# Softmax reciprocals on GpSimd's power instead of VectorE, in a fused attention and gated-MLP kernel

## The chip, the cores and the metric

The kernel runs on one core of one Trainium2 chip. The metric is the time of one execution on the device in microseconds (us). A core has TensorE (matrix products; PE, and PEld for its weight loads), VectorE (DVE), ScalarE (ACT), GpSimd (POOL) and SyncE (SP, which here only issues DMAs). Each works through its own instructions in order, and they wait for each other on semaphores.

## The reference

One input x of 2048 tokens by 512 channels goes through a layernorm, and three things are added: x itself, a sliding-window attention, and a gated MLP whose gate mixes tokens.

```python
xn = layernorm(x)
# attention: 32 heads of 16, each token looks at 8 tokens: itself and 2, 4, ... 14 before it
q, k, v = xn @ wqkv
logits  = einsum('bhsd,bhswd->bhsw', q, k_gathered) * 16 ** -0.5    # masked before token 0
attn    = softmax(logits)                                           # over the 8
A       = einsum('bhsw,bhswd->bhsd', attn, v_gathered) @ wo
# gated MLP
z  = gelu(xn @ w_in);  z1, z2 = z[..., :896], layernorm(z[..., 896:])
g  = einsum('ts,bsf->btf', w_sp, z2) + b_sp                         # 2048 x 2048
B  = (z1 * g) @ w_out
out = x + A + B
```

The matmuls take bf16 operands, with fp16 in some sums.

## The kernel before

The kernel is a list of tasks. Each task names its engine, the buffers that it reads and writes, an estimated duration (`est`, in ns) and a function that issues one or a few instructions. From the buffers the planner works out what must wait for what. The order of the tasks on each engine is written out by hand in `plan.orders`: five lists, for TensorE, ScalarE, VectorE, GpSimd and SyncE. The estimates only settle what the lists leave open.

Tokens are kept in 16 blocks of 128. The work goes through these stages:

- Layernorm of x (`bnst`, `bnag`, `rstd`, `norm`). `rstd` is a GpSimd power of one element per partition: the variance to the power -0.5 (line 657).
- Products with w_in and wqkv (`z2_`, `Q`, `K`, `z1_`, `V`). For the attention's logits VectorE multiplies Q with shifted K (`prod`, line 758) and adds up (`padd`, line 766); TensorE sums over the channels of a head (`lg`).
- The layernorm of z2, in four waves of four blocks (`zm`, `zq`, `ze`, `zv`, `zr`, `zb`, `zn`). `zr` is a GpSimd power of four elements per partition (line 934); `zb` (line 936, VectorE) reads its result.
- The softmax, in four groups of 512 tokens, 3 first and 0 last. VectorE takes the maximum over the eight window positions (`sm1`, `sm2`, `sm3`), subtracts it (`ssub`), ScalarE takes the exponential (`sexp`), VectorE adds the eight (`sz1`, `sz2`, `sz3`), takes the reciprocal of the sum (`srec`, line 847, 128 partitions by 128 sums) and multiplies (`sattn`).
- The spatial product with w_sp, in eight tiles of two output blocks. It is a fast scheme with seven products (`P1` to `P7`, 8 matmuls each) instead of eight; VectorE makes sums of z2 (`T1` to `T4`, line 962) and, for each tile, sums of the weights (`S13`, `S2`, `S4`, lines 982 to 988). It also takes two of the four results out of the PSUM (`g12`, `g22`) and multiplies the gate with z1 (`u`). A DMA transposes each `u` (`uT`).
- Beside each tile VectorE does the attention's weighted sum of V for two blocks: `pv` (line 1163), then halving sums `pva2048`, `pva1024` (line 1167) and `pvc` (line 1171), then a DMA transposes the result (`OTd`).
- The output blocks `out15` to `out0` on TensorE (lines 1225 and 1229) take the transposed attention times wo and the transposed `u` times w_out, onto x.

The sums Z and the reciprocals R of the softmax have one buffer each, shared by the four groups. So `sz3` of a group waits until the reciprocal of the group before it has read Z, and a reciprocal waits until `sattn` of the group before it has read R. In VectorE's list of before, the reciprocal of a group stands between its `sz3` and its `sattn`; group 3 comes at about 102 us, group 2 at 113, group 1 at 163 and group 0 at 189.

Of the kernel before, what the change touches and what calls it, by code (L numbers as in the profile page):

```python
# [14 lines left out]
class Plan:  # L15
# [291 lines left out]
ALU = mybir.AluOpType  # L307
ACTF = mybir.ActivationFunctionType
# [18 lines left out]
def build_kernel(nc, A_x, A_wqkv, A_wo, B_x, B_w_in, B_w_sp, B_b_sp, B_w_out, out, report=False, sched_kw=None,  # L327
                 cfg=None, emit=True):
    cfg = dict(DEFAULT_CFG, **(cfg or {}))
# [10 lines left out]
    FILL = cfg["fill"]  # L340
# [65 lines left out]

    foff = {}
    fb = 0
    for name, n in (("prime", 4), ("Z", 128), ("st6", NB * 9),
                    ("mv", NB * 2), ("rstd", NB), ("s1", 2 * NB), ("s2", NB), ("m2", NB), ("msq", NB),  # L410
                    ("rstd2", NB), ("nb2", NB), ("mhalf", 4), ("bias", NB), ("P5s", 2 * HF)):
        foff[name] = fb
        fb += n
    F32_E = fb
# [3 lines left out]
    with ExitStack() as es:  # L418
# [10 lines left out]
        def A(name, n, o2_=0):  # L429
            return ar[:, off[name] + o2_: off[name] + o2_ + n]  # L430
# [16 lines left out]
        R = plan.reg  # L447
# [101 lines left out]
        zeros = A("zeros", 512)  # L549
        maskt = A("maskt", 32)  # L550
        hm = A("hm", 32)
        mhalf = Fv("mhalf", 4)
# [53 lines left out]
        for which, eng in ((0, "sp"), (1, "sp")):  # L606
# [4 lines left out]
                writes=[(("wq", "wk")[which], c) for c in range(4)],  # L611
                name="ld%s" % ("qk"[which]))
# [7 lines left out]
        def filler(n, name, est, prio=None, reads=(), w=512):  # L620
# [6 lines left out]

        filler(cfg["warm"], "warm", 114.0 * cfg["warm"], w=146)

        T("act", lambda a: a.activation(Fv("prime", 4), mhalf, ACTF.Gelu_apprx_tanh), reads=["mhalf"], writes=["prime"],  # L630
          est=-1200, name="actprime", tbl="gelu")

        ring = [0]
# [201 lines left out]
        def softmax_tail(j):  # L835
# [4 lines left out]
              reads=[dk], writes=["Za"], est=c_dve(512, 2.0), name="sz1_%d" % j, prio=FILL)  # L840
            T("dve", lambda v: v.tensor_tensor(AC(off["Zb"], [[64, 4], [1, 64]]), AC(off["Za"], [[128, 4], [1, 64]]),
                                               AC(off["Za"] + 64, [[128, 4], [1, 64]]), ALU.add),
              reads=["Za"], writes=["Zb"], est=c_dve(256, 2.0), name="sz2_%d" % j, prio=FILL)
            T("dve", lambda v: v.tensor_tensor(FCa(foff["Z"], [[32, 4], [1, 32]]), AC(off["Zb"], [[64, 4], [1, 32]]),
                                               AC(off["Zb"] + 32, [[64, 4], [1, 32]]), ALU.add),
              reads=["Zb"], writes=["Z"], est=c_dve(128), name="sz3_%d" % j, prio=FILL)
            T("dve", lambda v: v.reciprocal(A("R", 128), Fv("Z", 128)), reads=["Z"], writes=["R"], est=960,
              name="srec%d" % j, prio=FILL)
            dv = AC(off["attn"] + d0, [[256, 4], [32, 8], [1, 32]])
            T("dve", lambda v: v.tensor_tensor(dv, dv, AC(off["R"], [[32, 4], [0, 8], [1, 32]]), ALU.mult),  # L850
              reads=["R"], writes=[dk], est=c_dve(1024, 2.0), name="sattn%d" % j, prio=FILL)
# [226 lines left out]
        for j in range(NJ):  # L1078
# [18 lines left out]
            if j == 1:  # L1097
# [5 lines left out]
                  name="biasf")  # L1103
# [141 lines left out]
        for t in range(NT):  # L1245
# [11 lines left out]
            if t >= 1:  # L1257
# [4 lines left out]
        plan.orders = [  # L1262
            """
                warm xTr0b fill0 xTr0a z2_0_0b z2_0_1b z2_0_0a xTr1a xTr1b z2_0_1a xNr z2_1_0a z2_1_0b z2_1_1a xTr2a
                xTr2b z2_1_1b z2_2_0a z2_2_0b xTr3a z2_2_1a xTr3b z2_2_1b z2_3_0a z2_3_1a z2_3_1b z2_3_0b K0_0 K0_3
                K0_1 Q0_1 K0_2 Q0_0 Q0_2 Q0_3 K1_0 Q1_0 Q1_1 Q1_2 K1_1 K1_2 K1_3 Q1_3 z2_4 z2_5 z2_6 z2_7 Q2_0 K2_0
                Q2_1 K2_1 Q2_2 K2_2 Q2_3 K2_3 z2_8 z2_10 z2_9 z2_11 Q3_1 K3_1 K3_0 K3_2 Q3_2 Q3_0 z2_12 z2_13 K3_3
                lg0_0 Q3_3 z1_14 z2_15 z2_14 z1_12 z1_13 z1_15 z1_11 z1_8 z1_10 z1_6 z1_7 z1_9 z1_5 z1_4 z1_2 z1_0
                z1_3 z1_1 V12 V13 V15 V14 lg2_0 V9 V10 V11 V6 V7 V4 V3 V8 V5 V1 V0 V2 P1_0 P5_0 P6_0 P2_0 P7_0 bits
                P3_0 P1_1 P4_0 P5_1 P6_1 P2_1 P3_1 P7_1 P1_2 P4_1 P2_2 P6_2 P5_2 P7_2 P3_2 out15_0 P4_2 out14_0 P1_3  # L1270
                P5_3 P6_3 P2_3 P7_3 P3_3 P1_4 P4_3 P5_4 P2_4 out13_0 P6_4 out12_0 P7_4 P3_4 out11_0 P1_5 P5_5 P4_4
                P6_5 out10_0 P2_5 P7_5 P3_5 P1_6 P4_5 out8_0 P6_6 P2_6 P5_6 P7_6 P3_6 P1_7 out9_0 out6_0 P5_7 P4_6
                out7_0 P6_7 out4_0 P3_7 P7_7 P2_7 out5_0 P4_7 out3_0 out2_0 out0_0 out1_1 out1_0 out1_2
            """.split(),
            """
                actprime ldw_in2a_1 ldw_in2b_1 ldx2 ctr0 xTe0b xTe0a xTe1a xTe1b xNe z2g0_0 xTe2a xTe2b z2g0_1 z2g1_0
                xTe3a xTe3b z2g2_1 z2g1_1 z2g2_0 z2g3_0 z2g3_1 z2s0 QKe0_1 z2s1 QKe0_0 QKe0_2 QKe0_3 z2s2 halo0_0
                QKe1_0 halo1_0 halo0_2 halo0_3 QKe1_1 QKe1_2 z2s3 halo1_1 QKe1_3 biasf halo0_1 z2g4 z2s4 z2g5 z2g6
                z2s5 z2g7 z2s6 QKe2_0 QKe2_1 z2s7 QKe2_2 QKe2_3 halo1_3 zn2 z2g8 halo1_2 z2g10 z2s8 halo2_2 z2g9 z2g11
                z2s9 QKe3_1 halo2_3 z2s10 QKe3_2 QKe3_0 z2s11 z2g12 z2g13 z2s12 lge0 QKe3_3 lge1 halo2_1 z1g14 z2g15  # L1280
                zn3 z2g14 z2s13 z1g12 z1g13 z2s14 z1g15 halo2_0 z1g11 zn6 z1g8 zn7 z1g10 z1g6 z2s15 z1g7 z1g9 zn1 z1g5
                zn4 z1g4 z1g2 zn0 z1g0 zn8 z1g3 zn5 Ve12 Ve13 zn9 Ve15 z1g1 lge2 lge3 Ve9 Ve10 Ve11 Ve14 zn10 zn11 Ve7
                Ve6 ldxr0 Ve8 Ve4 sexp3 Ve5 Ve2 cA_0 Ve1 Ve3 Ve0 cB_0 g11_0 sexp2 cE_0 cA_1 g21_0 cE_1 cB_1 g11_1
                sexp1 cA_2 g21_1 os14_0 os15_0 cB_2 cE_2 g21_2 g11_2 cA_3 cB_3 ldxr2 ldxr1 cE_3 fin15_0 g11_3 cA_4
                fin14_0 os13_0 os12_0 g21_3 cE_4 sexp0 fin13_0 cB_4 fin12_0 os11_0 ldxr3 st0_0_0 os10_0 ldxr4 st1_0_0
                g11_4 cA_5 g21_4 cB_5 fin10_0 fin11_0 os8_0 os9_0 g11_5 ldxr5 cE_5 cA_6 g21_5 cB_6 os6_0 fin8_0
                st2_0_0 os7_0 g11_6 cE_6 cA_7 fin9_0 ldxr6 os4_0 st3_0_0 g21_6 fin6_0 fin7_0 os5_0 cB_7 fin4_0 os2_0
                cE_7 os3_0 st4_0_0 g11_7 ldxr7 fin5_0 g21_7 fin3_0 os0_0 os1_1 st5_0_0 fin2_0 os1_0 st6_0_0 fin0_0
                os1_2 fin1_0 st7_0_0 fin1_2 st7_1_384
            """.split(),  # L1290
            """
                zeros steps0 steps1 bnst0 bnag0 ctr1 bnst1 bnag1 norm0 norm1 bnst2 bnag2 bnst3 norm2 bnag3 norm3 bnst5
                bnag5 norm5 bnst6 bnag6 bnst4 bnag4 bnst7 norm6 bnag7 norm4 bnst10 zm0_0 norm7 bnag10 zm0 zq0 bnst11
                bnst8 bnag11 bnst9 bnag8 prod0_1 prod0_0 bnag9 norm10 norm8 bnst14 norm11 bnag14 padd0_0 bnst12 norm9
                bnst13 bnag12 bnag13 bnst15 prod0_2 norm14 bnag15 padd0_1 ze0 norm12 zv0 norm13 prod0_3 zm1 norm15
                padd0_2 zb0 prod1_2 prod1_0 padd1_0 zq1 padd1_1 ze2 prod2_0 zm2 ze1 prod2_2 zv1 zq2 padd2_0 zb1 zv2
                prod3_2 padd2_1 zm3 prod3_0 zq3 ze3 zb2 padd3_0 zv3 T3_0 padd3_1 smask T1_0 T3_1 S13_0 T2_0 zb3 zn12
                zn13 zn14 T1_1 S2_0 zn15 S4_0 T3_3 T4_0 T2_1 T1_3 sm1_3 T2_3 sm2_3 sm3_3 T3_2 ssub3 T1_2 T4_3 T2_2
                T4_1 T4_2 sz1_3 sz2_3 sz3_3 sm1_2 srec3 sm2_2 sattn3 sm3_2 pv15 ssub2 pv14 sz1_2 g22_0 sz2_2 g12_0
                S13_1 sz3_2 S2_1 u14 sm1_1 srec2 S4_1 pva2048_0 sm2_1 u15 sm3_1 pva1024_0 ssub1 g12_1 g22_1 u12 pvc0  # L1300
                S13_2 sz1_1 S2_2 sattn2 S4_2 sz2_1 u13 pv12 pv13 sm1_0 sz3_1 g22_2 pva2048_1 sm2_0 g12_2 pva1024_1
                S13_3 pvc1 S2_3 pv11 pv10 S4_3 pva2048_2 u11 g22_3 S13_4 sm3_0 g12_3 u10 pva1024_2 S2_4 ssub0 S4_4
                pvc2 u8 pv9 pv8 sz1_0 pva2048_3 S13_5 pva1024_3 g22_4 pvc3 srec1 g12_4 u9 u6 sattn1 S2_5 pv6 pv7 S4_5
                sz2_0 pva2048_4 u7 pva1024_4 g22_5 sz3_0 pvc4 S13_6 g12_5 S2_6 pv4 pv5 S4_6 pva2048_5 u4 u5 pva1024_5
# [66 lines left out]
```

## Time and profile before

| | |
|---|---|
| median of 3 runs | 226.86 us (226.82 to 228.16) |
| profiled execution | 226.98 us, span 225.2 us |
| TensorE busy | 220.8 us (98%), granted clock 1.0 |
| VectorE busy | 209.0 us (93%), 246 instructions |
| ScalarE busy | 135.4 us (60%) |
| GpSimd busy | 36.2 us (16%), the last instruction at 84.6 us |
| VectorE reciprocals | 4, mean 950 ns |
| GpSimd powers of 128x1 | 16, mean 1056 ns (548 to 2571) |
| GpSimd powers of 128x4 | 4, mean 4303 ns (3330 to 5201) |

The span runs from the first to the last instruction of the profiled execution. Busy time is the time in which an engine has an instruction under way, which says nothing of what it waits for inside an instruction. Matmuls are pipelined, and their ends are modelled. VectorE's instructions are recorded with an overlap of some 0.08 us, so the step from one start to the next is a little shorter than a duration.

### The profile page before, as it was taken

The page shows a single profiled execution, that of the slowest core. Times are in us where ns is not written, and L with a number is a line of the kernel's source. Part 1 is how long each engine was busy: PE and PEld are TensorE (multiplying, and loading weights), DVE is VectorE, ACT ScalarE, POOL GpSimd, SP SyncE. Part 2 cuts the span into 40 slices and gives each one's busy share as a digit, 9 for nine tenths or more (in the row PEclk, how much of TensorE's full clock was granted, in tenths as well). Part 3 has the DMA queues.
Part 4 walks back from the last instruction along what each step waited for, and adds up shares of the span by engine and source line. Part 5 has one row for each costly group of instructions (what it writes and reads, how often), then busy time and mean ns, then how long its engine had stood idle before and what let it go on. Part 6 is the DMA issues. An engine that isn't in the chain of part 4 may idle for free.

```text
span 225.2 us, 3118 instructions
## 1 busy us (share of the span) xinstructions
PE 220.8 (98%) x1162; PEld 122.1 (54%) x1176; DVE 209.0 (93%) x246; ACT 135.4 (60%) x241; POOL 36.2 (16%) x35
## 2 busy tenths in 40 slices
PE   8999999999999999999999999999999999999995
PEld 6555555554677775665454445554454555444444
DVE  4699999999998999999999999999999999999910
ACT  4679899899999999985434211362425241244342
POOL 4445595000079106000000000000000000000000
PEclk9999999999999999999999999999999999999999
DMA  6995365850000005669997989849955994507272
GB/s 220 260 197 141 71 188 117 136 122 0 0 3 0 0 0 166 139 119 273 199 204 156 183 156 204 203 94 180 231 123 111 221 176 95 140 0 162 75 162 93
DMA packets 77400, 29.96 MB, mean 133 GB/s; under 512 B 68669, under 2 KB 75339, under 8 KB 77259
## 3 DMA queue, kind: packets, MB, share of 16 engines
q1 hardware_dynamic: 74250, 25.08, 54.2%
q10 hardware_dynamic: 3136, 4.69, 6.2%
q8 instruction: 9, 0.15, 0.3%
q14 instruction: 5, 0.04, 0.1%
HBM read 9.05 MB, written 2.10 MB: 49 GB/s over the span
## 4 chain that ended last, share of the span: by engine, by line
PE 56%; DVE 35%; issue 5%; POOL 2%; ACT 1%; DVEq 0%
PE ps L1023 32%; DVE arena L758 14%; PE ps L1229 11%; DVE arena L766 8%; PE ps L1225 6%; DVE arena L962 4%; PE ps L883 3%; POOL fpool L934 2%; PE ps L624 2%; PE ps L735 2%; DVE arena L1163 1%; DVE fpool L652 1%; DVE arena L982 1%; DVE arena L667 1%; DVE arena L945 1%
## 5 line engine op out<-in xcount | busy, mean ns | idle before, releaser
L1023 PE MATMUL ps<-arena 128*128 128x448 f16 (+1 forms) x448 | 87.3, 353 | 0.3 <-DVE arena L982 0.2
L1023 PEld LDWEIGHTS ps<-arena 128*128 128x128 f16 (+1 forms) x448 | 43.4, 98 | 42.6 <-DVE arena L1069 0.8
L1163 DVE TENSOR_TENSOR arena<-arena 128x4096 bf16<-128x4096 bf16 x16 | 36.0, 2291 | 0.0
L758 DVE TENSOR_TENSOR arena<-arena 128x8192 bf16<-128x8192 bf16 (+1 forms) x10 | 35.5, 3563 | 0.3 <-ACT arena L743 0.3
L1038 ACT ACTIVATE ps<-ps 128x448 f32<-128x448 f32 x16 | 8.4, 528 | 35.4 <-DVE arena L1065 17.8
L1167 DVE TENSOR_TENSOR arena<-arena 128x4096 bf16<-128x4096 bf16 (+1 forms) x16 | 28.1, 1757 | 0.0
L735 PE MATMUL ps<-arena 128*128 128x512 bf16 x123 | 27.7, 379 | 0.4 <-issue 0.2
L1229 PE MATMUL ps<-arena 128*128 128x512 bf16 (+2 forms) x125 | 26.9, 355 | 0.1
L766 DVE TENSOR_TENSOR arena<-arena 128x4096 bf16<-128x4096 bf16 (+1 forms) x9 | 26.9, 2987 | 0.0
L903 PE MATMUL ps<-arena 128*128 128x448 bf16 x128 | 24.5, 352 | 0.0
L934 POOL TENSOR_TENSOR fpool<-fpool 128x4 f32<-128x4 f32 x4 | 17.2, 4303 | 37.2 <-DVE fpool L928 26.3
L1041 ACT ACTIVATE arena<-ps,fpool 128x448 bf16<-128x448 f32 x16 | 10.0, 631 | 20.5 <-PE ps L1023 19.1
L903 PEld LDWEIGHTS ps<-arena 128*128 128x128 bf16 x128 | 18.5, 144 | 5.9
L735 PEld LDWEIGHTS ps<-arena 128*128 128x128 bf16 x128 | 14.4, 113 | 13.2 <-issue 0.4
L657 POOL TENSOR_TENSOR fpool<-fpool 128x1 f32<-128x1 f32 x16 | 16.8, 1056 | 13.6 <-DVE fpool L655 13.1
L1238 ACT ACTIVATE arena<-ps 128x512 bf16<-128x512 f32 (+2 forms) x17 | 9.4, 560 | 15.6 <-PE ps L1229 15.6
L860 PE MATMUL ps<-arena 128*128 128x448 bf16 x96 | 18.8, 352 | 0.0
L1229 PEld LDWEIGHTS ps<-arena 128*128 128x128 bf16 x126 | 11.9, 98 | 12.4
L743 ACT ACTIVATE arena<-ps 128x1024 bf16<-128x1024 f32 x16 | 15.9, 1022 | 3.1 <-PE ps L735 3.1
L1225 PE MATMUL ps<-arena 128*128 128x512 bf16 (+2 forms) x66 | 15.5, 353 | 0.3
L915 ACT ACTIVATE arena<-arena 128x896 bf16<-128x896 bf16 x16 | 15.2, 949 | 0.1
L909 ACT ACTIVATE arena<-ps 128x896 bf16<-128x896 f32 x16 | 14.3, 911 | 0.4 <-PE ps L903 0.2
(85 smaller groups left out, 243.4 us busy)
## 6 DMA issues: line engine op xcount, KB each, us to landing
arena<-in_A_x_dram ACTq DMA_DIRECT2D x8, 256.0 KB, 3.4
arena<-in_A_x_dram SPq DMA_DIRECT2D x15, 128.0 KB, 2.5
out_dram<-arena ACTq DMA_DIRECT2D x7, 256.0 KB, 3.1
arena<-arena SPq DMA_DIRECT2D x1, 1568.0 KB, 9.2
arena<-in_A_wqkv_dram SPq DMA_DIRECT2D x3, 512.0 KB, 4.6
arena<-in_B_w_in_dram SPq DMA_DIRECT2D x1, 896.0 KB, 4.9
arena<-in_B_w_out_dram SPq DMA_DIRECT2D x1, 896.0 KB, 5.1
arena<-arena SPq DMA_TRANSPOSE x40, 3.2
```

The costliest lines, as they stand in the source:

```text
L657: T("pool", lambda g: g.tensor_tensor(Fv("rstd", 1, b), Fv("mv", 1, 2 * b + 1), Fv("mhalf", 1), ALU.pow), reads=[("mv", b), "mhalf"], writ ...
L735: last = t.matmul(bank(k + which), AC(off["wqk"] + 1024 * dc + col0, [[4, 128]]), AC(off["xnT"] + dc * S + 512 * j, [[1, 512]]), start=(dc ...
L758: T("dve", lambda v: v.tensor_tensor(pbv, qb, kb, ALU.mult), reads=[(t_, c, j) for t_ in ("QT", "KT", "KTpad") for c in cs], writes=[("pb" ...
L766: T("dve", lambda v: v.tensor_tensor(av, av, bv, ALU.add), reads=[("pb", s_) for s_ in b], writes=[("pb", s_) for s_ in a], est=c_dve(4096 ...
L860: last = t.matmul(ps[:, 512 * (k + hf): 512 * (k + hf) + HF], AC(off["xnT"] + dc * S + 128 * b, [[1, 128]]), AC(off["w_in2"] + FH * dc + H ...
L903: lastm = t.matmul(ps[:, 512 * (k + hf): 512 * (k + hf) + HF], AC(off["xnT"] + dc * S + b, [[NTOK, 128]]), AC(off["w_in1"] + FH * dc + HF ...
L934: T("pool", lambda g: g.tensor_tensor(Fv("rstd2", 4, 4 * j), Fv("msq", 4, 4 * j), mhalf, ALU.pow), reads=[("msq", j), "mhalf"], writes=[(" ...
L1023: last = t_.matmul(pb_(k_), st(k), mv(k), start=(start and k == 0), stop=(k == 7), skip_group_check=True)
L1163: T("dve", (lambda iv, tv, av: lambda v: v.tensor_tensor(tv, iv, av, ALU.mult))(iv, tv, av), reads=[("attn", q // 4)] + [("V", i_) for i_ ...
L1167: T("dve", (lambda n: lambda v: v.tensor_tensor(AC(off["Vs"], [[4096, 2], [1, n]]), AC(off["Vs"], [[4096, 2], [1, n]]), AC(off["Vs"] + n, ...
L1225: t_.matmul(po, AC(off["OT"] + 1024 * (t % 3) + 512 * r_ + 128 * cc, [[1, 128]]), AC(off["wo"] + 512 * cc + c0, [[1, n]]), start=False, st ...
L1229: last = t_.matmul(po, AC(off["z1"] + FH * tb + 128 * fc, [[1, 128]]), AC(off["w_out"] + 512 * fc + c0, [[1, n]]), start=False, stop=(fc = ...
```

## The change

For groups 0, 1 and 2 the reciprocal becomes a GpSimd power with exponent -1: the exponent is a constant -1.0 in one new fp32 element per partition, read 128 times. Group 3 keeps VectorE's reciprocal. To make room, the buffer of the priming activation shrinks by two columns. The planner's estimate for the power is 20 us. All five lists are new, and were made with longer durations for the z2 powers than before; GpSimd's now ends with `srec2 srec1 srec0`, and VectorE's leaves a stretch of other work between `sz3` and `sattn` of these groups.

```diff
@@ DEFAULT_CFG
+    rpool=(0, 1, 2),
@@ build_kernel
-    for name, n in (("prime", 4), ("Z", 128), ("st6", NB * 9),
+    for name, n in (("prime", 2), ("Z", 128), ("st6", NB * 9),
...
-                    ("rstd2", NB), ("nb2", NB), ("mhalf", 4), ("bias", NB), ("P5s", 2 * HF)):
+                    ("rstd2", NB), ("nb2", NB), ("mhalf", 4), ("mone", 1), ("bias", NB), ("P5s", 2 * HF)):
...
+        T("pool", lambda g: g.memset(Fv("mone", 1), -1.0), writes=["mone"], est=110, name="mone", prio=2)
...
@@ softmax_tail
-            T("dve", lambda v: v.reciprocal(A("R", 128), Fv("Z", 128)), reads=["Z"], writes=["R"], est=960,
-              name="srec%d" % j, prio=FILL)
+            if j in cfg["rpool"]:
+                T("pool", lambda g: g.tensor_tensor(A("R", 128), Fv("Z", 128), FCa(foff["mone"], [[0, 128]]), ALU.pow),
+                  reads=["Z", "mone"], writes=["R"], est=20000, name="srec%d" % j)
+            else:
+                T("dve", lambda v: v.reciprocal(A("R", 128), Fv("Z", 128)), reads=["Z"], writes=["R"], est=960,
+                  name="srec%d" % j, prio=FILL)
@@ plan.orders, VectorE, around the moved steps (before)
-  ... S13_1 sz3_2 S2_1 u14 sm1_1 srec2 S4_1 pva2048_0 sm2_1 u15 sm3_1 pva1024_0 ssub1 g12_1 g22_1 u12 pvc0
-  S13_2 sz1_1 S2_2 sattn2 ... sm1_0 sz3_1 g22_2 ... pvc3 srec1 g12_4 u9 u6 sattn1 ...
-  sz3_0 pvc4 ... pva1024_5 srec0 S13_7 sattn0 ...
@@ the same (after)
+  ... sz3_2 sm1_1 S13_1 g12_0 sm2_1 S2_1 sm3_1 pv14 u14 ssub1 S4_1 pva2048_0 g22_1 sz1_1 S13_2 g12_1 S2_2 pva1024_0 u15 pvc0
+  S4_2 sz2_1 u12 u13 sm1_0 pv12 pv13 g12_2 sz3_1 pva2048_1 g22_2 sattn2 pva1024_1 S13_3 ... pv8 pv9
+  sattn1 pva2048_3 sz1_0 g22_4 sz2_0 pva1024_3 sz3_0 S13_5 g12_4 S2_5 u9 pvc3 u6 pv6 pv7 S4_5 pva2048_4
+  S13_6 pva1024_4 g22_5 S2_6 g12_5 S4_6 pvc4 u7 pv5 pv4 u4 pva2048_5 sattn0 ...
@@ plan.orders, GpSimd (after)
+  ... rstd12 rstd14 zr0 zr1 zr2 mask1 zr3 srec2 srec1 srec0
```

More of the change, by code (lines that the diff above doesn't have):

```diff
@@ L628, in build_kernel @@
         filler(cfg["warm"], "warm", 114.0 * cfg["warm"], w=146)
-        T("act", lambda a: a.activation(Fv("prime", 4), mhalf, ACTF.Gelu_apprx_tanh), reads=["mhalf"], writes=["prime"],
+        T("act", lambda a: a.activation(Fv("prime", 2), Fv("mhalf", 2), ACTF.Gelu_apprx_tanh), reads=["mhalf"], writes=["prime"],
           est=-1200, name="actprime", tbl="gelu")
@@ L1264, in build_kernel @@
                 warm xTr0b fill0 xTr0a z2_0_0b z2_0_1b z2_0_0a xTr1a xTr1b z2_0_1a xNr z2_1_0a z2_1_0b z2_1_1a xTr2a
[L1265 to L1273, printed above, removed]
+                xTr2b z2_1_1b z2_2_0a z2_2_0b xTr3a z2_2_1a xTr3b z2_2_1b z2_3_0a z2_3_1a z2_3_1b z2_3_0b K0_0 K0_1
+                K0_3 Q0_0 K0_2 Q0_1 Q0_2 Q0_3 K1_0 Q1_1 K1_1 Q1_0 K1_2 Q1_2 z2_4 Q1_3 K1_3 z2_7 z2_5 z2_6 K2_2 K2_0
+                Q2_0 K2_1 Q2_1 Q2_3 K2_3 Q2_2 z2_8 z2_10 z2_9 z2_11 K3_1 Q3_1 Q3_0 K3_2 Q3_2 K3_0 z2_12 z2_13 Q3_3
+                K3_3 lg0_0 z1_14 z2_15 z2_14 z1_13 z1_12 z1_15 z1_11 z1_8 z1_6 z1_10 z1_7 z1_5 z1_9 z1_2 z1_0 z1_4 V13
+                z1_1 V12 z1_3 V10 lg2_0 V11 V14 V15 V7 V6 V8 V4 V9 V5 V1 V2 V0 V3 P1_0 P5_0 P6_0 P2_0 P7_0 bits P3_0
+                P4_0 P1_1 P5_1 P6_1 P2_1 P7_1 P3_1 P1_2 P4_1 P6_2 P2_2 P5_2 P3_2 P7_2 P1_3 out14_0 P2_3 P4_2 out15_0
+                P6_3 P5_3 P7_3 P3_3 P1_4 P4_3 out12_0 P5_4 P2_4 P6_4 out13_0 P7_4 P3_4 out11_0 P4_4 P1_5 out10_0 P6_5
+                P5_5 P2_5 P7_5 P3_5 P1_6 P5_6 P4_5 P6_6 out8_0 P3_6 P2_6 P7_6 out9_0 P1_7 out6_0 P6_7 P5_7 P4_6 P7_7
+                P3_7 P2_7 out7_0 out5_0 out4_0 P4_7 out2_0 out3_0 out0_0 out1_1 out1_0 out1_2
             """.split(),
@@ L1276, in build_kernel @@
                 actprime ldw_in2a_1 ldw_in2b_1 ldx2 ctr0 xTe0b xTe0a xTe1a xTe1b xNe z2g0_0 xTe2a xTe2b z2g0_1 z2g1_0
[L1277 to L1289, printed above, removed]
+                xTe3a xTe3b z2g2_0 z2g2_1 z2g3_1 z2g1_1 z2g3_0 z2s0 z2s1 QKe0_0 z2s2 QKe0_1 QKe0_2 z2s3 QKe0_3 QKe1_1
@@ new lines, in build_kernel @@
+                QKe1_0 halo0_1 halo0_2 halo1_1 QKe1_2 halo0_3 z2g4 QKe1_3 z2s4 z2g7 halo0_0 z2g5 z2s5 z2g6 z2s6 QKe2_0
+                z2s7 QKe2_1 halo1_0 halo1_2 QKe2_3 QKe2_2 z2g8 halo1_3 z2s8 z2g10 z2g9 halo2_3 z2s9 z2g11 z2s10 QKe3_1
+                zn2 QKe3_2 QKe3_0 halo2_1 z2s11 z2g12 z2g13 zn7 QKe3_3 lge0 z2s12 z1g14 zn1 halo2_0 z2g15 z2g14 z2s13
+                z1g13 z1g12 zn6 z1g15 z1g11 z2s14 z1g8 z2s15 z1g6 halo2_2 lge1 z1g10 z1g7 biasf zn4 z1g5 z1g9 zn11 zn3
+                z1g0 z1g2 z1g4 zn9 Ve13 z1g1 Ve12 zn8 z1g3 zn10 lge2 lge3 Ve14 Ve11 Ve10 Ve15 zn0 Ve7 ldxr1 ldxr0 Ve8
@@ new lines, in build_kernel @@
+                Ve6 zn5 Ve9 Ve4 Ve2 Ve5 sexp3 cA_0 Ve1 cE_0 Ve3 Ve0 cB_0 sexp2 g11_0 cA_1 cB_1 os15_0 g11_1 cE_1 sexp1
+                cA_2 g21_0 cB_2 g21_1 cE_2 os14_0 g11_2 cA_3 fin15_0 fin14_0 cB_3 g11_3 cE_3 os12_0 ldxr2 st0_0_0
+                g21_2 cA_4 sexp0 g21_3 os13_0 cB_4 fin12_0 fin13_0 os10_0 os11_0 cE_4 ldxr4 ldxr3 g11_4 fin11_0 cA_5
+                cB_5 fin10_0 g21_4 st2_0_0 cE_5 os6_0 g11_5 os8_0 os9_0 st1_0_0 cA_6 cB_6 fin8_0 os7_0 ldxr6 ldxr5
+                cE_6 g11_6 g21_5 fin9_0 st3_0_0 cA_7 fin6_0 cB_7 os4_0 cE_7 os5_0 g21_6 ldxr7 fin7_0 g11_7 st4_0_0
@@ L1290, in build_kernel @@
+                os2_0 fin5_0 fin4_0 st5_0_0 os0_0 g21_7 os3_0 fin2_0 fin3_0 os1_1 os1_0 st6_0_0 fin0_0 os1_2 fin1_0
+                st7_0_0 fin1_2 st7_1_384
             """.split(),
             """
-                zeros steps0 steps1 bnst0 bnag0 ctr1 bnst1 bnag1 norm0 norm1 bnst2 bnag2 bnst3 norm2 bnag3 norm3 bnst5
-                bnag5 norm5 bnst6 bnag6 bnst4 bnag4 bnst7 norm6 bnag7 norm4 bnst10 zm0_0 norm7 bnag10 zm0 zq0 bnst11
-                bnst8 bnag11 bnst9 bnag8 prod0_1 prod0_0 bnag9 norm10 norm8 bnst14 norm11 bnag14 padd0_0 bnst12 norm9
@@ L1295, in build_kernel @@
[L1295 to L1304, printed above, removed]
@@ L1305, in build_kernel @@
-                srec0 S13_7 sattn0 g22_6 pvc5 g12_6 pv2 pv3 S2_7 pva2048_6 S4_7 pva1024_6 u3 pvc6 u2 pv1 pv0 g12_7
-                g22_7 pva2048_7 u0 pva1024_7 pvc7 u1 fin1_1
+                zeros steps0 steps1 bnst0 bnag0 ctr1 bnst1 bnag1 norm0 norm1 bnst2 bnag2 bnst3 norm2 bnag3 norm3 bnst4
+                bnag4 norm4 bnst6 bnag6 bnst5 norm6 bnag5 bnst7 bnag7 norm5 zm0_0 bnst9 norm7 bnag9 zm0 bnst8 zq0
+                bnst10 bnag8 bnag10 prod0_0 prod0_1 norm8 bnst11 norm9 bnag11 ze0 padd0_0 norm10 bnst12 norm11 bnst15
@@ new lines, in build_kernel @@
+                bnst13 bnag15 bnag13 prod0_2 zv0 bnag12 padd0_1 bnst14 norm13 prod0_3 zm1 bnag14 norm15 norm12 padd0_2
+                norm14 zq1 ze1 prod1_2 zv1 prod1_0 zb0 zm2 padd1_0 zb1 zq2 padd1_1 prod2_0 ze2 prod2_2 zm3 zv2 padd2_0
+                zq3 prod3_0 ze3 prod3_2 zb2 padd2_1 zv3 padd3_0 padd3_1 zn15 zn14 smask zn13 zn12 T3_2 S13_0 T1_2 S2_0
+                T2_2 T3_3 T1_3 T4_2 T3_0 T2_3 T4_3 S4_0 T1_0 sm1_3 T3_1 sm2_3 sm3_3 ssub3 T2_0 T1_1 T2_1 T4_0 T4_1
+                sz1_3 sz2_3 sm1_2 sz3_3 sm2_2 srec3 sm3_2 zb3 sattn3 ssub2 pv15 g22_0 sz1_2 sz2_2 sz3_2 sm1_1 S13_1
@@ new lines, in build_kernel @@
+                g12_0 sm2_1 S2_1 sm3_1 pv14 u14 ssub1 S4_1 pva2048_0 g22_1 sz1_1 S13_2 g12_1 S2_2 pva1024_0 u15 pvc0
+                S4_2 sz2_1 u12 u13 sm1_0 pv12 pv13 g12_2 sz3_1 pva2048_1 g22_2 sattn2 pva1024_1 S13_3 sm2_0 S2_3 sm3_0
+                pvc1 S4_3 ssub0 u10 pv11 pv10 g22_3 pva2048_2 u11 S13_4 g12_3 S2_4 pva1024_2 u8 pvc2 S4_4 pv8 pv9
+                sattn1 pva2048_3 sz1_0 g22_4 sz2_0 pva1024_3 sz3_0 S13_5 g12_4 S2_5 u9 pvc3 u6 pv6 pv7 S4_5 pva2048_4
+                S13_6 pva1024_4 g22_5 S2_6 g12_5 S4_6 pvc4 u7 pv5 pv4 u4 pva2048_5 sattn0 pva1024_5 g12_6 pvc5 S13_7
@@ L1307, in build_kernel @@
+                g22_6 S2_7 pv2 pv3 u5 S4_7 pva2048_6 u2 pva1024_6 u3 pvc6 g12_7 pv0 pv1 u0 g22_7 pva2048_7 pva1024_7
+                pvc7 u1 fin1_1
             """.split(),
             """
-                mhalf ident0 ident1 nident0 nident1 ktpad rstd0 rstd1 rstd2 rstd3 mask0 hm0 hm1 rstd5 hm2 rstd6 rstd4
-                rstd7 mask1 rstd10 rstd8 rstd11 rstd9 rstd14 rstd13 rstd12 rstd15 zr0 zr1 zr2 zr3
+                mhalf ident0 mone ident1 nident0 nident1 ktpad rstd0 rstd1 rstd2 rstd3 hm0 mask0 rstd4 rstd6 hm1 rstd5
@@ L1311, in build_kernel @@
+                rstd7 rstd9 hm2 rstd8 rstd10 rstd11 rstd13 rstd15 rstd12 rstd14 zr0 zr1 zr2 mask1 zr3 srec2 srec1
+                srec0
             """.split(),
             """
-                ldx0 ldx1 ldw_in2a_0 ldw_in2b_0 ldx3 ldx5 ldx6 ldx4 ldx7 ldk ldx10 ldx11 ldq ldx9 ldx8 xTd5 xTd6 xTd4
-                xTd7 ldx14 ldx13 ldx15 ldb ldx12 xTd10 xTd11 xTd8 xTd9 ldw_in1 xTd12 xTd13 w0_0 xTd15 xTd14 ldwv w0_1
-                ldwout Vzero pT3 pT2 pT1 pT0 w1_0 w1_1 Vhaloa w2_0 w2_1 Vhalob ldwo1 ldwo0 ldwo2 ldwo3 uT15 OTd0 uT14
@@ L1316, in build_kernel @@
-                w3_0 w3_1 uT13 uT12 w4_1 w4_0 OTd1 w5_0 w5_1 uT11 OTd2 uT10 uT8 w6_0 uT9 OTd3 w6_1 w7_0 uT6 uT7 w7_1
-                OTd4 uT4 uT5 OTd5 uT3 uT2 OTd6 uT0 OTd7 uT1 st7_1_192 st7_1_0
+                ldx0 ldx1 ldw_in2a_0 ldw_in2b_0 ldx3 ldx4 ldx6 ldx5 ldk ldx7 ldx9 ldq ldx8 ldx10 xTd4 xTd6 xTd5 xTd7
+                ldx11 ldx12 ldx15 ldb ldx14 ldx13 xTd9 xTd8 xTd10 xTd11 ldwv w0_0 xTd13 xTd15 xTd12 xTd14 ldw_in1 w0_1
+                ldwout pT3 pT2 Vzero pT0 pT1 w1_0 w1_1 Vhalob ldwo0 ldwo1 ldwo2 w2_0 w2_1 Vhaloa ldwo3 uT14 w3_0 OTd0
@@ L1318, in build_kernel @@
+                uT15 w3_1 w4_0 uT12 uT13 OTd1 w4_1 w5_0 uT10 uT11 OTd2 w5_1 w6_0 uT8 w6_1 uT9 OTd3 uT6 w7_0 OTd4 w7_1
+                uT7 uT4 uT5 OTd5 uT3 uT2 OTd6 uT0 OTd7 uT1 st7_1_192 st7_1_0
             """.split(),
```

## The prediction

> **What bounds the kernel now.** I read the busy shares first, then the table by stretches, the chain of waits, the groups of lines 657, 847 and 934, and last the timelines of VectorE and GpSimd side by side.
>
> ```profile
> PE 220.8 (98%) x1162; PEld 122.1 (54%) x1176; DVE 209.0 (93%) x246; ACT 135.4 (60%) x241; POOL 36.2 (16%) x35
> ...
> PE 56%; DVE 35%; issue 5%; POOL 2%; ACT 1%; DVEq 0%
> ...
> 105.00:125.00 20.00, 19.70 (x104) 9.63 (x103) 20.00 (x29) 8.21 (x13) 0.00 (x0) 1.00 1.02 204
> 125.00:145.00 20.00, 19.95 (x103) 10.02 (x103) 20.00 (x19) 4.84 (x9) 0.00 (x0) 1.00 0.85 180
> 145.00:165.00 20.00, 19.89 (x101) 9.88 (x102) 20.00 (x24) 7.64 (x13) 0.00 (x0) 1.00 0.77 175
> 165.00:185.00 20.00, 19.95 (x103) 10.08 (x103) 20.00 (x21) 7.43 (x15) 0.00 (x0) 1.00 0.75 148
> ```
>
> The stretch columns are length, then busy time and count of PE, PEld, DVE, ACT and POOL, then granted clock, DMA share and GB/s. From 105 us on, where the reciprocals in question stand, TensorE and VectorE are both full, and GpSimd does nothing. The chain's last 111 us is TensorE work without a gap, but each spatial product needs a weight sum (S13, S2, S4) that VectorE has just made. Set side by side, product P5 of tile 1 starts 0.05 us after its S13 ends, P6 of tiles 1 and 2 start 0.59 and 0.05 us after their S2, P3 of tile 3 starts 0.81 us after its S4. So neither engine has room: a stall of VectorE reaches TensorE within about 1 us, and work taken from VectorE alone can at most close the 1.3 us that TensorE idles between its first matmul (0.84) and its last end (222.96; busy 220.8).
>
> At the end the two meet again:
>
> ```profile
> 213.57 0.69 DVE L1171 TENSOR_TENSOR arena<-arena 128x1024 bf16<-128x1024 bf16 x1
> ...
> 214.29 1.23 SPq L1175 DMA_TRANSPOSE arena<-arena  x1
> ...
> 217.95 1.03 PE L1225 MATMUL ps<-arena 128*128 128x512 bf16 x4
> ```
>
> The last pvc sum ends at 214.26, its transpose is issued at once and lands 3.2 us later (median of these transposes), at about 217.5, and the output block that needs it starts at 217.7 to 217.95. VectorE's end has some 0.2 us of room before it moves the end of the kernel.
>
> **What a power costs.** A VectorE reciprocal stands in the groups at 0.95 us; start to next start it is 0.86 (102.15 to 103.01). No power of 128x128 is in the trace. The nearest rows are those of 128x1 and 128x4, beside VectorE's tensor_tensor of the same moment:
>
> ```profile
> 23.93 2.24 DVE L766 TENSOR_TENSOR arena<-arena 128x4096 bf16<-128x4096 bf16 x1
> ...
> 24.09 2.49 POOL L657 TENSOR_TENSOR fpool<-fpool 128x1 f32<-128x1 f32 x1 [1.01 <-DVE fpool L655]
> ...
> 68.82 4.42 DVE L758 TENSOR_TENSOR arena<-arena 128x8192 bf16<-128x8192 bf16 x1
> 73.16 2.29 DVE L766 TENSOR_TENSOR arena<-arena 128x4096 bf16<-128x4096 bf16 x1
> ...
> 63.43 5.20 POOL L934 TENSOR_TENSOR fpool<-fpool 128x4 f32<-128x4 f32 x1 [26.28 <-DVE fpool L928]
> 68.98 5.12 POOL L934 TENSOR_TENSOR fpool<-fpool 128x4 f32<-128x4 f32 x1 [0.35 <-DVE fpool L932]
> ```
>
> Read the ends, not the durations. The 128x1 power ends at 26.58, 0.41 us after the VectorE sum ends (26.17). The 128x4 power of 68.98 ends at 74.10, 0.87 us after the product before it ends (73.24). So the long spans are waits: a power gets nothing done while a VectorE tensor_tensor with two inputs in the SBUF runs. Behind its end, one element per partition takes 0.41 us and four take 0.87, that is (0.87 - 0.41) / 3 = 0.153 us per further element. A power of 128 elements is then 0.41 + 127 x 0.153 = 19.9 us. Bounds: 0.41 if length cost nothing, which the four-element row excludes, and 128 x 0.87 / 4 = 27.8 if it went at that row's mean. I take 19.9, the slope.
>
> **The change part by part.**
>
> Removed from VectorE: three reciprocals, 3 x 0.86 = 2.6 us.
>
> New lists: the second z2 power no longer holds VectorE up (0.90 us before line 936 in the waits; the new list puts a product, two tiny steps and a sum in between): 0.9 us. The rest of the lists reorders the same work. Adding up VectorE's list with the steps of the trace, S13 of tile 1 comes 2.3 us sooner, S2 of tile 2 3.7 sooner, S13 of tile 5 1.9 later, the last pvc and u 2.6 sooner (just the reciprocals). With TensorE full I count nothing for it.
>
> Added in the set-up: one memset of 128x1 on GpSimd, some 0.10 us like its neighbours there, before the first rstd power, for which GpSimd waits 1.8 us anyway. A priming activation of two columns instead of four: nothing.
>
> Moved: srec2, srec1, srec0 go to GpSimd's queue, last in it, so nothing queues behind them there but each other. They issue no DMA, and SP's queue isn't crossed; its transposes and TensorE follow VectorE's end. VectorE gets waits: sz3 of the next group writes Z, which the power reads, and sattn reads R. Behind sattn stand pv, S and u steps, all for TensorE. The new list puts cover there: between sz3 and sattn stand 24.8 us of VectorE steps for group 2, 24.1 for group 0, and 22.9 for group 1 (counted from sattn2, whose R must be read first); sz3_1 comes 21.8 us after sz3_2. Against 19.9 us plus a wait for the instruction in progress (up to 2.3) that is just enough. Without the cover each power would cost 19.9 - 0.86 us.
>
> What it does to VectorE meanwhile is the step that decides. The rows show that a power cannot read while a tensor_tensor reads. On a shared path the other direction must hold too while the power reads, and the cover consists of tensor_tensors. How long does the power read? The lower end: with four elements the hold cannot be seen beyond 0.15 us (a 128x32 sum at 87.14 takes 0.32 us, tiny sums around it 0.15 to 0.17), and the 73.16 sum keeps its 2.29 us while the power computes till 74.10. So reads run at least four elements ahead of the arithmetic, and the write-back collides with nothing. Were all 128 read ahead at that rate, the hold would be 32 x 0.15 = 4.8 us at most, and 0.15 us at least. The upper end: the whole 19.9. A read-ahead has to be stored somewhere, and 128 elements of two operands are 32 times what the row shows; I let it run 16 ahead, four times the row. The hold is then (128 - 16) x 0.153 = 17.1 us, nearer the long end.
>
> [...]
>
> **The sum.** Three holds of 17.1 us: +51.4. Reciprocals -2.6, z2 wait -0.9, room at the end -0.2. TensorE cannot run ahead by more than its 1 us, and it has kept its slack as the end is set by VectorE's last steps. Together +47.7 us. The profiled execution took 226.98 us (span 225.2 and 1.8 around it), so 274.7 us; the runs' median of 226.86 is 0.1 us lower, which I leave out.
>
> **The rivals.**
>
> (a) *No hold worth seeing; not slower.* Reads run ahead of the arithmetic by all 128 elements, or are given up whenever VectorE asks. For it: the four-element rows hold VectorE for 0.15 us at most. Against: 32 times as much must be stored or re-requested. Then the covers hide the powers, VectorE gains up to 3.5 us, and TensorE, full, lets at most 1.3 of it through: 225.7 to 227, say 226.3. It holds as long as a power stays under its cover of 21.8 to 24.8 us. Chance 0.25.
>
> (b) *The power is starved instead.* It reads in small pieces, and each piece waits for the VectorE instruction in progress; VectorE isn't held, but sz3 and sattn wait. A VectorE step averages 20.00 / 19 = 1.05 us between 125 and 145. With pieces of four elements, 32 x 1.05 = 33.7 us per power, over a cover of about 23.3 by 10.4: three times that, less 3.7, is +27.5, so 254.5 us. With pieces of 16 a power takes some 8 x 3 = 24 us and it vanishes (228). For it: at 84.55 a power missed the boundary between two sums (85.01) and waited through the second. Against: at 20.07 and 73.24 it got in between two of them at once. Chance 0.13.
>
> (c) *Held for the whole instruction*, 19.9 us: 3 x 19.9 - 3.7 = +56.0, so 283.0 us. Against it stands the read-ahead of four elements shown above. Chance 0.15. [...]
>
> (d) That the lists put the powers elsewhere than the words say: the instruction order of the changed kernel has exactly three 128x128 powers, last on GpSimd, and one reciprocal left on VectorE. What is left of this is a power priced otherwise (up to 27.8 us, over every cover; some 305 us). Chance 0.04.
>
> **How the numbers follow.** The hold with some read-ahead has 0.43; its own range, from 64 elements ahead (3 x 9.8 - 3.7 = +25.7, 252.7) to four (3 x 19.0 - 3.7 = +53.3, 280.3), is 252 to 281, and its middle choice 274.7 is the forecast. Cases on the other side hold 0.25, so the range reaches from their lower part over (b) to just beyond (c): 225.8 to 285. About 1% is what a measurement of this kernel can tell from no change (the runs lie within 0.6%). Faster by more than that, under 224.6, needs more than TensorE's 1.3 us of idle time: 0.02. Within 1%: case (a) but for that, and the mild end of (b): 0.25. Slower: 0.73.
>
> **What would show it.** In the profile after: three GpSimd rows of 128x128 at about 20 us (a slope of 0.153 right); inside each, one VectorE tensor_tensor stretched to some 17 us or an equal idle time before it, and TensorE waiting on VectorE for nearly as long; VectorE's busy time without stretches near 206.4. If VectorE's tensor_tensors keep their 0.6 to 2.3 us under the powers, the step from exclusion to a hold is wrong and (a) or (b) holds, told apart by waits before sz3_1 and sattn. A stretch far under 17 us says the read-ahead was too small.

## The result: 3.3% slower, and one wait explains it

The changed kernel took 234.92 us (median of 6; 233.51 to 235.51) against 227.53 us for the kernel before in the same comparison: ratio 1.0331, 95% interval 1.0305 to 1.0357. Its profiled execution took 234.94 us with a span of 233.2, 8.0 us more than the one of before. The sign was as forecast. The size was not: 274.7 us had been predicted, 47.7 us more than before.

The page of the changed kernel, busy shares, the slices of VectorE, GpSimd and the clock, and the group of the new powers:

```profile
PE 222.9 (96%) x1163; PEld 123.0 (53%) x1176; DVE 208.0 (89%) x243; ACT 135.1 (58%) x241; POOL 113.9 (49%) x39
...
DVE  4799999999999999999999999990699999998910
...
POOL 4345586440095350003999299999279990000000
PEclk9999999999999999999999999999859999999999
...
L850 POOL TENSOR_TENSOR arena<-fpool 128x128 bf16<-128x128 f32 x3 | 72.9, 24308 | 34.4 <-DVE fpool L846 29.6
```

VectorE is as full as before but for one hole (slice 28), and right behind the hole TensorE's clock falls for two slices. There is one hole, where three stretches of 17 us had been forecast. The three powers one by one, in GpSimd's timeline of the changed kernel (start, duration, then line and shapes):

```profile
108.84 20.84 POOL L850 TENSOR_TENSOR arena<-fpool 128x128 bf16<-128x128 f32 x1 [24.08 <-DVE fpool L846]
134.52 30.45 POOL L850 TENSOR_TENSOR arena<-fpool 128x128 bf16<-128x128 f32 x1 [4.83 <-DVE arena L856]
170.45 21.63 POOL L850 TENSOR_TENSOR arena<-fpool 128x128 bf16<-128x128 f32 x1 [5.47 <-DVE fpool L846]
```

Two are near the forecast of 19.9 us for a power. The second lasts 30.5 and outlives its cover. Who waited, among VectorE's and TensorE's own waits, and VectorE's timeline at that place:

```profile
DVE arena L856 <- POOL arena L850: 7.7, 1, 7.7
...
PE ps L1029 <- DVE arena L1075: 6.3, 1, 6.3
```

```profile
155.06 2.28 DVE L1169 TENSOR_TENSOR arena<-arena 128x4096 bf16<-128x4096 bf16 x1
165.01 0.69 DVE L856 TENSOR_TENSOR arena<-arena 128x1024 bf16<-128x1024 bf16 x1 [7.67 <-POOL arena L850]
```

VectorE stands for 7.67 us before sattn1 (line 856), which reads the second power's result. TensorE then runs dry for 6.3 us, waiting for g22_4 (line 1075), and restarts at a lower clock, as its timeline and the table by stretches (length, then PE, PEld, DVE, ACT, POOL, clock, DMA) show:

```profile
157.02 3.19 PE L1029 MATMUL ps<-arena 128*128 128x448 f16 x16
...
168.89 5.58 PE L1029 MATMUL ps<-arena 128*128 128x448 f16 x16 [6.30 <-DVE arena L1075]
```

```profile
165.00:170.00 5.00, 1.11 (x4) 0.45 (x5) 4.99 (x6) 0.00 (x0) 0.00 (x0) 0.69 0.00 0
170.00:175.00 5.00, 5.00 (x18) 2.15 (x17) 5.00 (x9) 0.50 (x1) 4.55 (x1) 0.63 0.34 74
175.00:180.00 5.00, 5.00 (x27) 2.50 (x26) 5.00 (x4) 1.64 (x5) 5.00 (x1) 1.00 0.91 179
```

Sixteen matmuls take 5.58 us behind the hole and 3.19 ahead of it; the granted clock is 0.69 and 0.63 and then 1.00 again. In shorter stretches it is 0.50 from 166.9 to 173.7 us: it fell 4.3 us into the idle time (TensorE's last matmul ends at 162.59) and was full again 4.9 us after the restart at 168.89. Together TensorE has 6.3 us idle and 2.1 us more busy time (222.9 against 220.8), 8.4 us in all, for the 8.0 us that the span grew.

Why is the second power 10 us longer? VectorE's timeline of the changed kernel around its start:

```profile
133.77 0.67 DVE L856 TENSOR_TENSOR arena<-arena 128x1024 bf16<-128x1024 bf16 x1
134.37 1.21 DVE L1173 TENSOR_TENSOR arena<-arena 128x2048 bf16<-128x2048 bf16 x1
135.50 1.21 DVE L988 TENSOR_TENSOR arena<-arena 128x2048 f16<-128x2048 bf16 x1
...
139.38 0.61 DVE L1053 TENSOR_TENSOR arena<-arena 128x896 bf16<-128x896 bf16 x1
139.92 4.48 DVE L1169 TENSOR_TENSOR arena<-arena 128x4096 bf16<-128x4096 bf16 x2
144.32 0.67 DVE L1075 SCALAR_TENSOR_TENSOR arena<-ps,fpool 128x448 bf16<-128x448 f32 x1
```

From 134.37 to 144.40 VectorE runs eleven tensor_tensors with two SBUF inputs (two-input instructions from here on), each started some 0.08 us before the one ahead of it ends. The next instruction, g22_3, reads the PSUM. The power ends at 164.97, which is 20.57 us behind 144.40. The third power ends at 192.07, 20.57 us behind 171.50, where g12_4 (a PSUM reader too) follows S13_5. The first ends at 129.68, 20.59 us behind the boundary at 109.10; a boundary is the moment at which one VectorE instruction ends and the next takes over:

```profile
108.68 0.42 DVE L820 TENSOR_TENSOR arena<-arena 128x512 bf16<-128x512 bf16 x1
109.02 1.42 DVE L988 TENSOR_TENSOR arena<-arena 128x2048 f16<-128x2048 bf16 x1
```

So each power ends 20.6 us behind a boundary, and the rest of its time lies ahead of it. Theory A: a power's reads wait until VectorE's run of two-input instructions is broken, and from then on it needs 20.6 us. Theory B: the second power is slowed along its whole way, by its company or its data, and the 20.57 is chance. Theory A has an exception from the start: both instructions at 109.10 (sm1_1 and S13_1) are two-input, and the first power got in between them.

### The profile page after: what moved, and what is told of

Same layout as the page of the kernel before. It is cut to its first block, busy times and chain, and to the rows that moved or that the text cites. A ratio compares the mean times of both kernels' runs of the same rounds, so it can differ in the third digit from the quotient of the medians.

```text
span 233.2 us, 3117 instructions
## 1 busy us (share of the span) xinstructions
PE 222.9 (96%) x1163; PEld 123.0 (53%) x1176; DVE 208.0 (89%) x243; ACT 135.1 (58%) x241; POOL 113.9 (49%) x39
## 4 chain that ended last, share of the span: by engine, by line
PE 68%; DVE 14%; POOL 13%; issue 3%; ACT 2%; DVEq 0%
PE ps L1029 15%; POOL arena L850 13%; PE ps L737 12%; PE ps L909 10%; PE ps L866 8%; PE ps L1235 7%; PE ps L721 5%; PE ps L1231 4%; DVE arena L1173 3%; PE ps L889 3%; DVE arena L1169 3%; PE ps L626 2%; DVE arena L988 1%; PE ps L795 1%; DVE arena L1075 1%
## 5 line engine op out<-in xcount | busy, mean ns | idle before, releaser
L1029 PE MATMUL ps<-arena 128*128 128x448 f16 (+1 forms) x448 | 89.0, 359 | 6.3 <-DVE arena L1075 6.3
L850 POOL TENSOR_TENSOR arena<-fpool 128x128 bf16<-128x128 f32 x3 | 72.9, 24308 | 34.4 <-DVE fpool L846 29.6
L1029 PEld LDWEIGHTS ps<-arena 128*128 128x128 f16 (+1 forms) x448 | 44.4, 99 | 49.6 <-DVE arena L1075 6.8
L940 POOL TENSOR_TENSOR fpool<-fpool 128x4 f32<-128x4 f32 x4 | 18.4, 4604 | 25.6 <-DVE fpool L938 25.6
L909 PE MATMUL ps<-arena 128*128 128x448 bf16 x128 | 24.9, 353 | 0.0
L866 PE MATMUL ps<-arena 128*128 128x448 bf16 x96 | 19.0, 352 | 0.0
```

The costliest lines, as they stand in the source:

```text
L850: T("pool", lambda g: g.tensor_tensor(A("R", 128), Fv("Z", 128), FCa(foff["mone"], [[0, 128]]), ALU.pow), reads=["Z", "mone"], writes=["R" ...
L866: last = t.matmul(ps[:, 512 * (k + hf): 512 * (k + hf) + HF], AC(off["xnT"] + dc * S + 128 * b, [[1, 128]]), AC(off["w_in2"] + FH * dc + H ...
L909: lastm = t.matmul(ps[:, 512 * (k + hf): 512 * (k + hf) + HF], AC(off["xnT"] + dc * S + b, [[NTOK, 128]]), AC(off["w_in1"] + FH * dc + HF ...
L940: T("pool", lambda g: g.tensor_tensor(Fv("rstd2", 4, 4 * j), Fv("msq", 4, 4 * j), mhalf, ALU.pow), reads=[("msq", j), "mhalf"], writes=[(" ...
L1029: last = t_.matmul(pb_(k_), st(k), mv(k), start=(start and k == 0), stop=(k == 7), skip_group_check=True)
```

## The experiments

Each experiment starts from the changed kernel unless its heading says otherwise. The kernel before, run beside them, had medians of 227.01 us (beside e1 to e4) and 226.95 us (beside e5 to e8).

**e1: another instruction where the second power starts**

```diff
 VectorE's list:
-  ... sz3_1 pva2048_1 g22_2 sattn2 pva1024_1 S13_3 ...
+  ... sz3_1 pva2048_1 sattn2 g22_2 pva1024_1 S13_3 ...
```

> The changed kernel with one step of VectorE's list moved: g22_2, which reads the PSUM, stands behind sattn2 instead of ahead of it, so it is the instruction that runs when the second power (group 1) starts. Theory A (a power's reads wait until VectorE's run of two-input SBUF instructions is broken; after that it needs 20.6 us and holds nobody up): the second power falls from 30.5 to about 20.7 us, the 7.7 us wait before sattn1 goes, TensorE keeps its clock, 225.5 to 227.5 us. Theory B (the second power is slowed all along its way, by the VectorE instructions it runs beside or by its group's data): still about 30 us, wait of 7 to 8 us, 234 to 235 us.

Measured: 225.84 us, ratio to before 0.9944 (0.9923 to 0.9965). GpSimd's timeline:

```profile
108.70 20.85 POOL L850 TENSOR_TENSOR arena<-fpool 128x128 bf16<-128x128 f32 x1 [24.07 <-DVE fpool L846]
133.79 20.72 POOL L850 TENSOR_TENSOR arena<-fpool 128x128 bf16<-128x128 f32 x1 [4.24 <-DVE arena L856]
162.54 21.63 POOL L850 TENSOR_TENSOR arena<-fpool 128x128 bf16<-128x128 f32 x1 [8.04 <-DVE fpool L846]
```

The second power starts inside g22_2 now and falls from 30.45 to 20.72 us, by moving one VectorE step over another. VectorE has no wait before sattn1, and TensorE's busy time is 220.8 us at full clock. This is what theory A expected; B falls. This version is also faster than the kernel before, by 0.8 us at least on the interval.

**e2: the new lists alone**

```diff
-    rpool=(0, 1, 2),
+    rpool=(),
 VectorE's list: + srec2 behind sz3_2, srec1 behind sattn2, srec0 behind sz3_0; GpSimd's: without them
```

> The new lists with all four reciprocals on VectorE: srec2 behind sz3_2, srec1 behind sattn2, srec0 behind sz3_0; no 128x128 power. Theory A and B: the power's wait is the whole loss, so 226.5 to 228 us, no VectorE wait before sattn1. Rival (the new lists themselves cost): over 230 us.

Measured: 227.68 us, ratio 1.002 (1.0 to 1.0041), no VectorE wait before sattn1. The lists bring nothing by themselves. Against them the three unstarved powers of e1 bring 1.8 us (227.68 - 225.84); 2.6 us of reciprocals had been taken off VectorE.

**e3: a longer run of two-input steps for the third power**

```diff
 VectorE's list:
-  ... sz3_0 S13_5 g12_4 S2_5 u9 pvc3 u6 pv6 pv7 S4_5 ...
+  ... sz3_0 S13_5 S2_5 u9 pvc3 pv6 pv7 g12_4 u6 S4_5 ...
```

> The changed kernel with VectorE's steps behind sz3_0 reordered: S13_5 S2_5 u9 pvc3 pv6 pv7 and only then g12_4 and u6. The third power (group 0), which took 21.6 us, now starts into a run of some 7 us of two-input SBUF instructions. Theory A: it lasts 20.6 us behind the end of that run, up to 28 us (less if it gets in at a boundary inside the run), and VectorE waits up to 4 us before sattn0. Theory B: about 21 us, no wait before sattn0. The second power stays at about 30 us in both.

Measured: 241.0 us (a single run). The third power was not starved: it lasted 21.63 us again, and the second 30.46. On the face of it this speaks against A. VectorE's timeline shows how it got in:

```profile
172.29 1.22 DVE L988 TENSOR_TENSOR arena<-arena 128x2048 f16<-128x2048 bf16 x1
173.54 0.77 DVE L992 TENSOR_TENSOR arena<-arena 128x1024 f16<-128x1024 f16 x1
174.24 0.61 DVE L1053 TENSOR_TENSOR arena<-arena 128x896 bf16<-128x896 bf16 x1
```

S2_5 (line 992) reads what S13_5 (line 988) has just written. It starts 0.03 us behind its end (173.51) instead of 0.08 ahead of it, and lasts 0.77 us instead of 0.68. The power ended at 194.08, 20.57 us behind 173.51: it got in at this gap, which the edit itself had made. But this was also the first boundary that the power met, and e4 shows that a power can get in there without a gap; so e3 doesn't decide. Of the extra 6 us against the changed kernel 2.0 are there before the first power starts (110.84 against 108.84). The rest isn't a wait for a power, which is 7.7 us as in the changed kernel: TensorE idles 3.3 us once more, its clock is at 0.50 again behind that (180.9 to 184.2 us), and VectorE waits 2.7 us before line 1075. That the moved g12_4 causes this is likely, but no run shows it.

**e4: forty small powers as probes, in the kernel before**

```diff
+        for i_ in range(40):
+            T("pool", (lambda i_: lambda g: g.tensor_tensor(Fv("st6", 16, 16 * (i_ % 9)), Fv("rstd", 16),
+                                          FCa(foff["mhalf"], [[0, 16]]), ALU.pow))(i_), ..., name="probe%d" % i_)
 GpSimd's list: + probe0 ... probe39 at the end
```

> The kernel before with forty powers of 128x16 added at the end of GpSimd's list, one behind the other from about 90 us on; nobody reads their results. Each is a sample of when a power's reads get in. By the slope of the rows of before (0.153 us an element) one needs 0.41 + 15 x 0.153 = 2.7 us behind the moment its reads get in. Theory A: ends lie about 2.7 us behind the end of a run of two-input VectorE instructions, spacings vary between 2.7 us and 10 us, VectorE loses under 1 us in all and the time stays within 1%. Theory B: spacings lie evenly around one value, whatever VectorE runs. The hold that was forecast: VectorE instructions stretched by up to 2 us each, 240 us and more.

Measured: 254.48 us (a single run), but only because GpSimd's chain now ends last: with nobody in the way a probe takes 2.89 us, and some took far longer, so the forty ran 29 us beyond TensorE's last matmul. The expected time was therefore wrong. TensorE is done at 223.6 us of the span, and VectorE lost little: its busy time is 209.4 us against 209.0, and no instruction beside a probe is stretched by more than 0.05 us against the same one before. Three of the probes:

```profile
123.61 10.34 POOL L1245 TENSOR_TENSOR fpool<-fpool 128x16 f32<-128x16 f32 x1
...
148.73 16.31 POOL L1245 TENSOR_TENSOR fpool<-fpool 128x16 f32<-128x16 f32 x1
...
198.69 2.89 POOL L1245 TENSOR_TENSOR fpool<-fpool 128x16 f32<-128x16 f32 x1
```

Taking 2.69 us off the end of each, an estimate close to the 2.7 us expected, gives the moment its reads got in, to within 0.1 us. Six probes stayed out for two or more boundaries between two-input instructions, up to twelve; five of them got in at the next instruction that is not a tensor_tensor (zb3 or zn12 behind it, g22_2, g22_3, g22_4, the reciprocal srec0), and one at a gap of 0.03 us like that of e3, behind seven lost boundaries. But fifteen others got in at the very first boundary between two two-input instructions, or 0.1 us behind it. So a run does not shut a power out for certain. A probe that lost the first boundary lost all others of its run, but that isn't a rule either: the 128x4 power at 84.55 in the kernel before lost the boundary at 85.01 and got in at the next, at 87.21, again between two-input instructions. What decides isn't known.

**e5 and e6: break the run with a short instruction of one input, or of two**

```diff
+            if j == 1:
+                T("dve", lambda v: v.reciprocal(Fv("st6", 64, 72), Fv("st6", 64)), ..., name="xtra")      # e5
+                T("dve", lambda v: v.tensor_tensor(Fv("st6", 64, 72), Fv("st6", 64), Fv("st6", 64), ALU.add), ...)   # e6
 VectorE's list: ... sattn2 pva1024_1 xtra S13_3 ...
```

> The changed kernel with one more VectorE instruction, 64 elements per partition, right behind pva1024_1, some 2 us into the run that starves the second power: a reciprocal, which has one SBUF input. Its result is not used. Theory A: the power's reads get in beside it, the power lasts about 22 us instead of 30.5 (20.6 behind the end of pva1024_1), the 7.7 us wait goes, 226 to 228 us. Theory B: no change, 30 us, wait of 7 us, 235 us.

> The same with a sum of 64 elements in that place instead of the reciprocal: also short, but with two SBUF inputs. Its result is not used. Theory A: the run is not broken, the power lasts 30 to 31 us, VectorE waits 7 to 8 us, 234 to 236 us. A rival to A (any short instruction or any shift of the timing frees the power): as with the reciprocal, about 22 us and 226 to 228 us.

Measured: e5 225.81 us, ratio 0.9939 (0.9919 to 0.9959); e6 233.83 us, ratio 1.0297 (1.025 to 1.0343). The second power and VectorE's two steps at its start (pva1024_1 and the added one), in e5, then in e6:

```profile
134.34 21.63 POOL L853 TENSOR_TENSOR arena<-fpool 128x128 bf16<-128x128 f32 x1 [4.84 <-DVE arena L859]
...
134.18 1.22 DVE L1176 TENSOR_TENSOR arena<-arena 128x2048 bf16<-128x2048 bf16 x1
135.32 0.54 DVE L850 RECIPROCAL fpool<-fpool 128x64 f32<-128x64 f32 x1
```

```profile
134.11 30.59 POOL L853 TENSOR_TENSOR arena<-fpool 128x128 bf16<-128x128 f32 x1 [4.84 <-DVE arena L859]
...
133.95 1.21 DVE L1176 TENSOR_TENSOR arena<-arena 128x2048 bf16<-128x2048 bf16 x1
135.09 0.22 DVE L850 TENSOR_TENSOR fpool<-fpool 128x64 f32<-128x64 f32 x1
```

Same place, same 64 elements. With one SBUF input the power gets in at the boundary (its end, 155.97, is 20.57 us behind pva1024_1's), with two it stays out till g22_3, and the wait of 7.7 us is back. In both, and in the changed kernel, the power starts 0.15 or 0.16 us behind the start of pva1024_1, so a shift of the timing does not explain the difference. The reciprocal is also longer than the sum (0.54 against 0.22 us), but length alone doesn't let a power in: the run has sums of 2.28 us that kept it out. So the kind of the instruction decides here.

**e7 and e8: which power costs**

```diff
-    rpool=(0, 1, 2),
+    rpool=(0, 2),      # e7; srec1 on VectorE behind sattn2
+    rpool=(1,),        # e8; srec2 and srec0 on VectorE behind their sz3
```

> The changed kernel with the power for groups 0 and 2 alone; group 1 is back on VectorE's reciprocal, right behind sattn2. Theory A: both powers 20.7 to 21.7 us, no VectorE wait, 226 to 227.5 us: between the lists alone (227.7) and the version with the moved g22_2 (225.8). Theory B: the same.

> The changed kernel with the power for group 1 alone; groups 0 and 2 are on VectorE's reciprocal, behind their sz3. Theory A: that power lasts about 30.5 us and VectorE waits 7 to 8 us before sattn1, 235 to 237 us: the whole loss comes from this one. Rival (the loss comes from three powers together): a third of it, 229 to 230 us.

Measured: e7 226.07 us, ratio 0.9957 (0.9933 to 0.9982), powers of 20.85 and 21.63 us; e8 235.12 us, ratio 1.0341 (1.029 to 1.0392), its one power 30.47 us and the wait 7.7. The whole loss belongs to the second power; the other two bring 1.6 us against the lists alone (227.68 - 226.07).

## Why the prediction was wrong

That the kernel became slower was forecast for a reason that did not happen. One swapped step (e1) makes it faster with all three powers in place, so the right sign was luck; and 234.9 us lies far below the 252 to 281 us of the hold that was forecast.

- **What bounds the kernel: right.** A wait of 7.7 us on VectorE became 6.3 us of TensorE idle and 8.0 us of span. That TensorE would let at most 1.3 us of a gain through was close: e1 gained 1.2 us (227.01 to 225.84) for 2.6 taken off VectorE.
- **The price of a power: right.** 19.9 us by the slope; 20.6 measured from the moment the reads get in.
- **The cover: right for two of three.** 24.8 and 24.1 us hid powers of 20.8 and 21.6; 22.9 did not hide 30.5. The wait for getting in was put at one instruction in progress, at most 2.3 us; this step failed too. It was 9.9 us for the second power, a whole run of instructions.
- **The hold: this step failed.** The term was 17.1 us, three times; no run shows it. What was measured is 0.2 us, once. S13_1, which starts as the first power's reads get in (109.02 above), takes 1.42 us instead of 1.22, and no other VectorE instruction of the changed kernel is stretched by as much beside the powers: for the 20 us that follow, the two-input sums keep their durations (1.21 us for the next S13, 2.28 for a pv). How the power reads its 128 elements no row shows. That a power gets nothing done while a two-input tensor_tensor runs, as the prediction read the rows of before, holds only until its reads are in (20.57 us behind that it ended, whether VectorE ran on all the way, as beside the third, or stood for 7.67 of them, as beside the second). The prediction's lower end (0.15 us) was the right one. Choosing an end by how much would have to be stored had no row behind it. The row that the lower end was read from was no hold either: the 128x32 sum takes 0.31 us in the changed kernel too, with no power running.
- **Rival (b) had the direction.** The power is the one that is kept out, and VectorE waits later at sattn (7.67 us). Its mechanism does not show: no time is lost in pieces, each power ends 20.57 to 20.59 us behind one boundary. The row at 84.55, cited for it, was this starvation in small: out at one boundary, in at the next.
- **Missing: TensorE's clock.** A wait of 7.7 us, less the 2.6 and 0.9 us saved, would be +4.2 us by the prediction's own terms. It was 8.0 because the 3.5 us saved on VectorE did not make up for the wait: 6.3 us of it reached TensorE, and the lower clock behind it cost 2.1 us more.

Of the exclusion that the prediction started from, the runs show one direction: in e6 the added two-input instruction left the power out (30.59 us), where the one with a single SBUF input in e5 let it in (21.63 us). The other direction, on which the hold and rival (c) rest, no run shows beyond the 0.2 us: the first power had VectorE's sums run beside it for 20 us.

## What to carry to other kernels

Work moved to GpSimd beside a full VectorE can have to wait until its reads get in, as the second power did (30.45 us): start it where VectorE runs something with one SBUF input (a reciprocal here, 21.63 us) or a PSUM input (g22_2 in e1, 20.72 us), and count its time from there. A cover that is just long enough can fail by the whole length of a run of two-input instructions (9.9 us here), and one swapped step (e1) turned a loss of 3.3% into a gain of 0.6%. When a cost can only be bounded from both sides and the sides are 0.15 and 19.9 us apart, the forecast should be two cases, not a value between them.

## What was not expected of the hardware

A 128x128 power of two fp32 operands held VectorE up for 0.2 us out of 20.6. A waiting GpSimd read stayed out for up to twelve boundaries between back-to-back two-input VectorE instructions (a probe of 2.89 us took 16.31); another got in at a gap of 0.03 us. In fifteen other samples it got in at the first boundary; what decides that stays open.
